# Four-step blocks of a decayed attention summed by VectorE's transposing reduction in place of TensorE's first burst

## The chip, the cores and the metric

One core of one Trainium2 chip. The metric is device time in microseconds (us) of one execution; profiles come from executions of the same program. PE is TensorE (PEld its weight loads), DVE is VectorE, ACT is ScalarE; L463 is line 463 of the kernel that the profile belongs to, so the same statement has another number in each kernel (L656, L706, L707 and L710 are all the MLP's first product).

## The reference

```python
# r, k, w, v: (4 batches, 8 heads, 768 steps, 48 channels)
for t in range(S):
    cur = u * k_t (x) v_t                     # outer product
    y_t = r_t . (state + cur)
    state = w_t[:, None] * state + k_t (x) v_t
# y as (3072, 384), then an MLP with exact Gelu:
out = gelu(y @ w_in) @ w_out                  # w_in (384, 2048), w_out (2048, 384)
```

## The kernel before

Time is cut into eight blocks, x = 0 to 7. For each, an attention part makes a matrix of r·k products with decays inside chunks of 64 steps, a state and y; an MLP then runs on y. The two are woven together: while the MLP of block x-1 runs, the attention of block x is taken forward by one piece at each "slot". The MLP's steps are 16 groups of six products (`h_ps`, each group followed by a Gelu), then the products with `w_out`. Only two banks hold `h_ps`, so group three needs the first Gelu.

From x = 2 on, the decayed products come in "quarters": at h = 1, 4 and 16, blocks of 4h steps are cut into four, and one burst of 96 matmuls makes the products between different quarters. The diagonal (step with itself) is a sum over channels on VectorE.

```python
QUARTERS = (1, 4, 16)
...
        if x >= 2:
            for q in range(qs):                                   # r * u * k, the diagonal
                nc.vector.scalar_tensor_tensor(out=kx[:, z], in0=r[:, z], scalar=u_sb[:, q:q + 1], in1=k[:, z], ...)
            nc.vector.tensor_reduce(out=diag_sb, in_=kx..., op=ALU.add, apply_transpose=True)
            yield
        # (cut) tot[2], tot[4], ...: products of w over 2, 4, ... steps
            def plain(h):                                         # copies of r into the right-hand side kx
                for z, f in ((s0[:, :, :, 0:h], 1), (s1[:, :, :, 0:h], 2), (s2, 3)):
                    nc.scalar.copy(out=z, in_=r4[:, :, :, f, :])
            def lay_out(h): ...                                   # two VectorE products, L442 and L443
            plain(1)
            lay_out(1)
            yield
            for h in QUARTERS:
                ...                                               # at h == 1: four small products place the diagonal (L456)
                            nc.tensor.matmul(d[...], lhsT=kc[...], rhs=rx[...], start=True, stop=True)   # the burst, L463
                nc.vector.tensor_mul(z, s0, ...)                  # r and k scaled for the next h
                ...
                        nc.vector.copy_predicated(out=an[...], mask=..., data=data)
                yield
...
        place = [...] if x == 1 else [0, 7, 11, 14, 16, 17, 17, 19, 20]      # steps for this block's pieces
        place_next = [40, 42] if x == 1 else [20, 22]                        # steps for the next block's preparation
```

## Time and profile before

| | before |
|---|---|
| median, lowest, highest (3 runs) | 626.23, 625.59, 627.41 us |
| span of the profiled run, granted clock | 625.5 us, 0.997 |
| PE / DVE / ACT busy | 97% / 70% / 30% |
| bursts of 96 matmuls, x = 2 to 7 | three a block, 2.14 us each |

### The profile page before, as it was taken

The numbers are of one execution on the slowest core, as the hardware profiler recorded it, in microseconds if no ns is written. First come the engines' busy times: TensorE is split into PE (matmuls) and PEld (weight loads), VectorE is DVE, ScalarE is ACT, GpSimd is POOL, SyncE is SP. The second block draws the span as 40 slices with busy tenths as digits, with TensorE's granted clock in tenths as the row PEclk, the third lists the DMA queues.
The fourth block names the chain that finished last, engine by engine and source line by source line (L and its number), as shares of the span: only waits on it lengthen the run. The fifth ranks groups of instructions, "written<-read, shape, count | busy, mean of one in ns | idle before, by whom it ended". The sixth has DMA issues, their size and how long they took to land.

```text
span 625.5 us, 16932 instructions
## 1 busy us (share of the span) xinstructions
PE 607.6 (97%) x7462; PEld 456.8 (73%) x7481; DVE 436.3 (70%) x802; ACT 186.0 (30%) x397; POOL 7.6 (1%) x29
## 2 busy tenths in 40 slices
PE   8798999989999999999999999999999999999997
PEld 4565666555689667996689667996689767995694
DVE  8987999798776777668776777677676777340120
ACT  2136556033224222223224232123234233112200
POOL 4000000000000000000000000000000000000000
PEclk9999999999999999999999999999999999999999
DMA  4576348002042214213042113212042002010001
GB/s 158 168 272 253 104 153 291 28 24 89 3 104 74 57 40 90 65 42 89 2 91 88 41 56 73 62 56 83 15 89 87 8 1 39 9 42 7 1 1 38
DMA packets 50505, 46.78 MB, mean 75 GB/s; under 512 B 31616, under 2 KB 35840, under 8 KB 50432
## 3 DMA queue, kind: packets, MB, share of 16 engines
q1 hardware_dynamic: 33120, 29.33, 14.8%
q10 hardware_dynamic: 17312, 16.37, 9.6%
q8 instruction: 59, 0.97, 0.6%
q14 instruction: 14, 0.11, 0.1%
HBM read 36.24 MB, written 4.72 MB: 65 GB/s over the span
## 4 chain that ended last, share of the span: by engine, by line
PE 81%; DVE 12%; issue 3%; DMA 2%; ACT 1%; SPq 0%; DVEq 0%; ACTq 0%
PE h_ps L656 35%; PE o_ps L676 29%; PE d L463 6%; PE o_ps L790 3%; DVE rkw L388 2%; PE d L353 2%; PE y_ps L571 2%; PE y_ps L589 2%; DVE e L291 2%; PE kv_ps L539 2%; DVE a_sb L396 1%; DMA raw<-in_w_in_dram 1%; PE warm L185 1%; DVE w_out_sb L295 1%; DMA xT<-ysb 1%
## 5 line engine op out<-in xcount | busy, mean ns | idle before, releaser
L656 PE MATMUL h_ps<-xT,w_in_sb 128*128 128x384 f32 x768 | 256.6, 491 | 0.4 <-DMA xT<-ysb 0.4
L656 PEld LDWEIGHTS h_ps<-xT,w_in_sb 128*128 128x128 f32 x768 | 144.3, 191 | 96.8 <-ACT xT L602 0.9
L659 ACT ACTIVATE g<-h_ps 128x384 f32<-128x384 f32 (+1 forms) x128 | 57.7, 451 | 216.4 <-PE h_ps L656 200.0
L494 DVE COPY_PREDICATED a_sb<-quarter,d 128x384 f32<-128x384 uint8 x162 | 82.4, 550 | 3.7
L676 PE MATMUL o_ps<-t,s 128*128 128x192 f32 x480 | 82.9, 329 | 0.0
L676 PEld LDWEIGHTS o_ps<-t,s 128*128 128x128 f32 x480 | 78.0, 190 | 0.8
L476 DVE TENSOR_TENSOR rkw<-rkw,tot_sb 128x768 f32<-128x768 f32 x18 | 17.3, 959 | 42.6 <-PE d L463 42.6
L463 PEld LDWEIGHTS d<-kx,rkw 64*64 64x64 f32 x1728 | 37.2, 135 | 9.1 <-issue 7.3
L463 PE MATMUL d<-kx,rkw 64*64 64x96 f32 x1728 | 40.7, 248 | 2.3 <-DVE kx L443 2.3
L790 PE MATMUL o_ps<-w_out_sb,g 128*128 128x384 f32 x128 | 42.7, 490 | 0.0
L437 ACT COPY kx<-rkw 128x384 f32<-128x384 f32 x54 | 31.3, 643 | 29.6 <-PE d L463 21.3
L676 PE MATMUL o_ps<-w_out_sb,g 128*128 128x192 f32 x224 | 39.3, 329 | 0.0
L676 PEld LDWEIGHTS o_ps<-w_out_sb,g 128*128 128x128 f32 x224 | 36.7, 190 | 2.2
L790 PEld LDWEIGHTS o_ps<-w_out_sb,g 128*128 128x128 f32 x128 | 23.9, 190 | 16.1 <-DVE o_sb L796 0.6
L669 DVE TENSOR_TENSOR s<-g 128x512 f32<-128x512 f32 x14 | 9.4, 672 | 29.9 <-ACT g L659 29.9
L676 PE MATMUL o_ps<-t,g 128*128 128x192 f32 x160 | 27.7, 327 | 0.2 <-ACT rkw L661 0.2
L676 PE MATMUL o_ps<-w_out_sb,s 128*128 128x192 f32 x160 | 27.6, 326 | 0.0
L353 PEld LDWEIGHTS d<-rkw 64*64 64x64 f32 x1152 | 18.7, 135 | 11.7 <-issue 5.8
L676 PEld LDWEIGHTS o_ps<-t,g 128*128 128x128 f32 x160 | 26.2, 190 | 0.5 <-ACT rkw L661 0.5
L676 PEld LDWEIGHTS o_ps<-w_out_sb,s 128*128 128x128 f32 x160 | 26.3, 190 | 0.0
L602 ACT COPY xT<-y_ps 48x384 f32<-48x384 f32 x46 | 21.7, 473 | 14.0 <-issue 12.4
L353 PE MATMUL d<-rkw 64*64 64x64 f32 (+1 forms) x1152 | 21.3, 222 | 4.4 <-DVE rkw L388 1.6
(109 smaller groups left out, 591.5 us busy)
## 6 DMA issues: line engine op xcount, KB each, us to landing
rkw<-in_rkw_dram ACTq DMA_DIRECT2D x45, 256.0 KB, 2.8
raw<-in_w_out_dram SPq DMA_DIRECT2D x8, 768.0 KB, 4.4
raw<-in_w_in_dram SPq DMA_DIRECT2D x7, 768.0 KB, 7.5
out_dram<-o_sb SPq DMA_DIRECT2D x21, 192.0 KB, 1.9
v_in<-in_v_dram ACTq DMA_DIRECT2D x5, 584.0 KB, 3.7
rkw<-in_rkw_dram SPq DMA_DIRECT2D x8, 288.0 KB, 3.6
rkw<-in_rkw_dram SPq DMA_DIRECT2D x9, 256.0 KB, 7.5
rkw<-kx SPq DMA_DIRECT2D x48, 48.0 KB, 2.1
```

The lines of the kernel that those rows point to most:

```text
L291: nc.vector.scalar_tensor_tensor(out=e, in0=hi, scalar=0x80000000, in1=e, op0=ALU.bitwise_and, op1=ALU.bitwise_or)
L353: nc.tensor.matmul(d[half[p], g, n * width:(n + 1) * width], lhsT=kc[half[g], b, i, p], rhs=right(half[g], b, i, p), start=True, stop=True)
L388: nc.vector.tensor_mul(rk, rk, tt)
L437: nc.scalar.copy(out=z, in_=r4[:, :, :, f, :])
L463: nc.tensor.matmul(d[half[p], g, i * 3 * C // 2:(i + 1) * 3 * C // 2], lhsT=kc[half[g], (n + i) // NI, (n + i) % NI, p], rhs=rx[half[g], 2 ...
L476: nc.vector.tensor_mul(z, z, t2[:, :, 1:2].to_broadcast(z.shape))
L494: nc.vector.copy_predicated(out=an[:, :, :, :, (a + 1) * h:], mask=mask.to_broadcast(data.shape), data=data)
L602: copy(out=xT[s, pair, :].rearrange("p (i c t) -> p c i t", c=2, t=C), in_=y[s])
L656: nc.tensor.matmul(h_ps, lhsT=w_in_sb[:, f // FI, j, f % FI * 128:(f % FI + 1) * 128], rhs=xT[:, j, :], start=(j == 0), stop=(j == NJ - 1))
L659: nc.scalar.activation(out=gs[group][:, f % FG, 0:t], in_=h_ps[:, 0:t], func=AF.Gelu)
L676: nc.tensor.matmul(o, lhsT=lhs(j), rhs=rhs(j), start=start and j == 0, stop=(j == HF - 1), skip_group_check=True)
L790: nc.tensor.matmul(o, lhsT=block(i, f // HF, f % HF), rhs=w_out_sb[:, f, :], start=(f == 0), stop=(f == NF - 1))
```

## The change

The intent: blocks of four steps are small enough that VectorE can make their ten products per block (step with itself, one, two and three steps apart) by multiplying shifted k and r and summing over channels with its transposing reduction. Eight small products put the sums in place. So the first burst is not needed, and `QUARTERS` starts at 4. The core of the diff:

```diff
-QUARTERS = (1, 4, 16)
+QUARTERS = (4, 16)
+FINE = 4
+        r4, k4, w4 = (z.rearrange("p (m a) -> p a m", a=FINE) for z in (r, k, w))
+        def transposed_sums(o, e, n):
+            nc.vector.tensor_reduce(out=fine_sb[:, e, 0:n]..., in_=kx[...], op=ALU.add, apply_transpose=True)
+        def apart(e, n):                                  # k times r, e steps apart
+            nc.vector.tensor_mul(kx[...].rearrange("p (a m) -> p a m", a=n), k4[:, 0:n], r4[:, e:e + n])
+        if x >= 2:
+            places_of = [apart(1, 3)]
+            times(k4[:, 0:2], w4[:, 1:3])
+            places_of.append(apart(2, 2))
+            times(k4[:, 0:1], w4[:, 2:3])
+            places_of.append(apart(3, 1))
+            yield
+            for e, place in enumerate(places_of, 1):
+                transposed_sums(place, e, FINE - e)
+            times(k4[:, 0:3], w4[:, 3:4]...)              # k and r scaled for h = 4
+            times(r4[:, 3:4], w4[:, 2:3])
+            times(r4[:, 1:2], w_0)
+            times(r4[:, 2:4], w_01...)
-            plain(1)
-            lay_out(1)
+            plain(FINE)
+            lay_out(FINE)
-                if h == 1:   # four small products for the diagonal
+                if h == FINE:
+                    for a in range(FINE):
+                        for g in range(2):
+                            nc.tensor.matmul(fine_ps[g][:, a * n_b:], lhsT=places[half[g], a], rhs=fine_sb[half[g], 0:FINE - a, a], ...)
# (cut) masks, and the predicated copies of the fine sums
-        place = [...] if x == 1 else [0, 7, 11, 14, 16, 17, 17, 19, 20]
+        place = [...] if x == 1 else [4, 9, 12, 14, 15, 15, 18, 19]
-        place_next = [40, 42] if x == 1 else [20, 22]
+        place_next = [34, 36, 38] if x == 1 else [20, 22, 24] if x % 2 == 0 else [20, 22, 27]
```

More of the change, by code (lines that the diff above doesn't have):

```diff
@@ L102 @@
     p1_alone = bufs[0][:, ALL + NF * 128:ALL + NF * 128 + DM // 2]
-    diag_sb = bufs[0][:, 3 * ALL - NP * T // 32:]
+    SPARE = ALL + NF * 128 + DM // 2
+    fine_sb = bufs[0][:, SPARE:SPARE + FINE * FINE * NPART * NI].rearrange("p (e a n) -> p e a n", e=FINE, a=FINE)
+    places = bufs[0][:, 3 * ALL - FINE * 128:].rearrange("p (a r) -> p a r", a=FINE)
     def load_first():
@@ L195 @@
     q_ints = [wk.tile([128, DM // 2], I32, name=name, bufs=1) for name in ("p1", "u2", "u3")]
-    s_qs = {h: q_ints[0][:, i * C:(i + 1) * C] for i, h in enumerate(QUARTERS)}
+    s_qs = {h: q_ints[0][:, i * C:(i + 1) * C] for i, h in enumerate((1,) + QUARTERS)}
     nc.gpsimd.iota(row, pattern=[[0, C]], base=0, channel_multiplier=1)
@@ L221 @@
     m_qs = {}
+    t_all, t_block = q_ints[1][:, 2 * C:3 * C], q_ints[2][:, 2 * C:3 * C]
+    nc.gpsimd.iota(t_all, pattern=[[1, C]], base=0, channel_multiplier=0)
+    nc.gpsimd.iota(t_block, pattern=[[1, C // FINE], [0, FINE]], base=0, channel_multiplier=0)
     for i, h in enumerate(QUARTERS):
@@ L228, with make_fine @@
             nc.gpsimd.iota(m_qs[h, a], pattern=[[4, C // 4 // h], [0, (3 - a) * h]], base=a, channel_multiplier=0)
+    fine_mask, later = (const.tile([128, C], U8, name=name) for name in ("fine_mask", "later"))
+    def make_fine():
+        nc.vector.tensor_tensor(out=fine_mask, in0=s_qs[FINE], in1=t_block, op=ALU.is_equal)
+        nc.vector.tensor_tensor(out=later, in0=t_all, in1=s_qs[1], op=ALU.is_ge)
+        nc.vector.tensor_tensor(out=fine_mask, in0=fine_mask, in1=later, op=ALU.bitwise_and)
+        nc.gpsimd.memset(places, 0.0)
+        for z in range(4):
+            o = slice(z * 32, (z + 1) * 32)
+            v = places[o]
+            v = bass.AP(tensor=v.tensor, offset=v.offset, ap=[v.ap[0], [128 + 1, FINE], [FINE, 32]])
+            nc.gpsimd.tensor_copy(out=v, in_=ident[o, o].unsqueeze(1).to_broadcast([32, FINE, 32]))
     def make_quarter_masks():
+        make_fine()
         for (h, a), m_q in m_qs.items():
@@ L235 @@
     make_identity(nc, ident)
-    both = const.tile([128, 2, C], F32, name="both")
-    nc.gpsimd.memset(both, 0.0)
-    for z in range(4):
-        o = slice(z * 32, (z + 1) * 32)
-        for i in range(2):
-            nc.gpsimd.tensor_copy(out=both[o, z // 2, i * 32:(i + 1) * 32], in_=ident[o, o])
     tot_sb = const.tile([128, NP * T], F32, name="tot_sb")
@@ L316, in attention @@
         xT = xT_of[x]
+        r4, k4, w4 = (z.rearrange("p (m a) -> p a m", a=FINE) for z in (r, k, w))
+        n_m = n_u // FINE
+        def transposed_sums(o, e, n):
+            nc.vector.tensor_reduce(out=fine_sb[:, e, 0:n].rearrange("p a n -> p (a n)"),
+                                    in_=kx[:, o:o + n * n_m].rearrange("p (m j) -> p m j", j=32),
+                                    axis=mybir.AxisListType.X, op=ALU.add, apply_transpose=True)
+        def apart(e, n):
+            o = sum(FINE - i for i in range(1, e)) * n_m
+            nc.vector.tensor_mul(kx[:, o:o + n * n_m].rearrange("p (a m) -> p a m", a=n), k4[:, 0:n], r4[:, e:e + n])
+            return o
         if x >= 2:
             for q in range(qs):
-                z = slice(q * T, (q + 1) * T)
-                nc.vector.scalar_tensor_tensor(out=kx[:, z], in0=r[:, z], scalar=u_sb[:, q:q + 1], in1=k[:, z],
+                m_q = slice(q * T // FINE, (q + 1) * T // FINE)
+                nc.vector.scalar_tensor_tensor(out=kx[:, 0:n_u].rearrange("p (a m) -> p a m", a=FINE)[:, :, m_q],
+                                               in0=r4[:, :, m_q], scalar=u_sb[:, q:q + 1], in1=k4[:, :, m_q],
                                                op0=ALU.mult, op1=ALU.mult)
-            nc.vector.tensor_reduce(out=diag_sb, in_=kx[:, 0:n_u].rearrange("p (m j) -> p m j", j=32), axis=mybir.AxisListType.X,
-                                    op=ALU.add, apply_transpose=True)
+            transposed_sums(0, 0, FINE)
             yield
@@ L342, in attention, with times @@
             at_tot += nb
-        if x < 2:
+        if x >= 2:
+            def times(z, by):
+                nc.vector.tensor_mul(z, z, by)
+            places_of = [apart(1, 3)]
[6 more added lines that the diff above has]
+                transposed_sums(place, e, FINE - e)
+            w_0, w_01 = w4[:, 0:1], tot[2].rearrange("p (m two) -> p two m", two=2)[:, 0:1]
+            times(k4[:, 0:3], w4[:, 3:4].to_broadcast([128, 3, n_m]))
+            times(r4[:, 3:4], w4[:, 2:3])
+            times(r4[:, 1:2], w_0)
+            times(r4[:, 2:4], w_01.to_broadcast([128, 2, n_m]))
+        else:
             yield
@@ L450, in quarters @@
                 banks = [ps.tile([128, 2, BANK], F32, name="d", tag="d", bufs=3) for _ in range(0, np_ * NI, 4)]
-                if h == 1:
-                    halves_of = diag_sb.rearrange("p (n c z) -> p n c z", c=2, z=2)
-                    for g in range(2):
-                        for c in range(2):
-                            nc.tensor.matmul(banks[-1][half[c], g, 6 * C:6 * C + 2 * np_ * NI], lhsT=both[:, g, :],
-                                             rhs=halves_of[:, :, c], start=True, stop=True)
+                if h == FINE:
+                    n_b = np_ * NI
+                    fine_ps = [banks[-1][:, g, 6 * C:6 * C + FINE * n_b] for g in range(2)]
+                    for a in range(FINE):
+                        for g in range(2):
+                            nc.tensor.matmul(fine_ps[g][:, a * n_b:], lhsT=places[half[g], a], rhs=fine_sb[half[g], 0:FINE - a, a],
+                                             start=(a == 0), stop=True, skip_group_check=True)
                 ds = []
@@ L495, in quarters @@
                         o += w_q
-                if h == 1:
-                    data = banks[-1][:, :, 6 * C:6 * C + 2 * np_ * NI].rearrange("p g (n z) -> p g n z", z=2)
-                    data = data.unsqueeze(4).to_broadcast([128, 2, np_ * NI, 2, C // 2])
-                    mask = masks[0].rearrange("p (z t) -> p z t", z=2).unsqueeze(1).unsqueeze(1)
-                    nc.vector.copy_predicated(out=at.rearrange("p g n (z t) -> p g n z t", z=2),
-                                              mask=mask.to_broadcast(data.shape), data=data)
+                if h == FINE:
+                    mask = fine_mask.rearrange("p (m b) -> p m b", b=FINE).unsqueeze(1)
+                    for g in range(2):
+                        data = fine_ps[g].rearrange("p (b n) -> p n b", n=n_b)
+                        data = data.unsqueeze(2).to_broadcast([128, n_b, C // FINE, FINE])
+                        nc.vector.copy_predicated(out=at[:, g].rearrange("p n (m b) -> p n m b", b=FINE),
+                                                  mask=mask.to_broadcast(data.shape), data=data)
                 yield
@@ L844 @@
     for x in range(1, NX):
-        place = [1, 2, 4, 7, 9, 11, 13, 15, 17, 20, 24, 32] if x == 1 else [0, 7, 11, 14, 16, 17, 17, 19, 20]
-        place_next = [40, 42] if x == 1 else [20, 22]
+        place = [1, 2, 4, 7, 9, 11, 13, 15, 18, 20, 26, 32] if x == 1 else [4, 9, 12, 14, 15, 15, 18, 19]
+        place_next = [34, 36, 38] if x == 1 else [20, 22, 24] if x % 2 == 0 else [20, 22, 27]
         loads = load(x + 1, nc.scalar if x > 1 else nc.sync)
-        times = range(20, 30) if x == 1 else (2, 3, 4, 5, 15, 16, 17, 19, 20, 21)
+        times = range(20, 30) if x == 1 else (2, 3, 4, 5, 13, 14, 15, 17, 18, 19)
         following = attention(x + 1, 0) if x + 1 < NX else iter(())
@@ L853 @@
         for step, _ in enumerate(mlp(x - 1)):
-            if x == 1 and step == 2 * NF + 2:
+            if x == 1 and step == 2 * NF - 4:
                 make_quarter_masks()
```

## The prediction

> **What bounds the kernel now.** I read the page's busy line first, then the chain that ended last in order of time, then VectorE's timeline around one hand-over between two time blocks, then durations by line.
>
> The busy line, then pieces of the chain (start, duration, engine, tile, line):
>
> ```profile
> PE 607.6 (97%) x7462; PEld 456.8 (73%) x7481; DVE 436.3 (70%) x802; ACT 186.0 (30%) x397; POOL 7.6 (1%) x29
> ```
> ```profile
> 137.03 0.97 DVE kx L443
> 138.13 3.06 PE d L463 x96
> ...
> 487.97 1.94 PE h_ps L656 x6
> 490.26 2.14 PE d L463 x96
> 492.40 13.74 PE h_ps L656 x42
> 506.14 2.14 PE d L463 x96
> 508.28 7.94 PE h_ps L656 x24
> 516.22 2.14 PE d L463 x96
> ```
>
> TensorE is busy 97% and from 138 us on the chain is TensorE nearly alone. So TensorE's work is the time there, and a change helps by what it takes off TensorE, as long as no other engine falls behind. Each of the six later blocks (x = 2 to 7) has three bursts of products, 2.14 us each, between groups of h_ps (6 instructions, 1.98 us a group). The change deletes the first burst. The one exception is the first hand-over, where TensorE waited for VectorE (L443) until 138.13.
>
> VectorE has 30% idle, but where it lies decides. Timeline of VectorE, around the hand-over at 488 us:
>
> ```profile
> 471.80 0.36 DVE L716 TENSOR_TENSOR u<-o_ps,p 128x192 f32<-128x192 f32 x1 [0.91 <-PE o_ps L676]
> ...
> 480.21 0.36 DVE L725 TENSOR_TENSOR u<-o_ps,p 128x192 f32<-128x192 f32 x1 [1.60 <-PE o_ps L676]
> 480.67 0.62 DVE L728 TENSOR_TENSOR o_sb<-o_sb,u 128x192 f32<-128x192 f32 x2
> 482.81 0.36 DVE L737 TENSOR_TENSOR o_sb<-o_ps,u 128x192 f32<-128x192 f32 x1 [1.51 <-PE o_ps L676]
> 483.09 0.95 DVE L341 TENSOR_TENSOR tot_sb<-rkw 128x768 f32<-128x768 f32 x1
> 484.07 1.71 DVE L341 TENSOR_TENSOR tot_sb<-tot_sb 128x384 f32<-128x384 f32 x5
> 485.69 0.86 DVE L442 TENSOR_TENSOR kx<-rkw 128x384 f32<-128x384 f32 x1
> 486.66 0.96 DVE L443 TENSOR_TENSOR kx<-kx,rkw 128x768 f32<-128x768 f32 x1
> ```
>
> The reader is to see that VectorE prepares the next block between the MLP's additions, and was done at 487.6, when TensorE wanted the result at 490.2: about 2.6 us to spare. Whatever is added between L716 and the first products of the next block has that room, no more.
>
> Last, one line of the kernel in its two forms, by source line (minimum/median/maximum ns): with steps of four elements (h = 1), and in runs of four or more.
>
> ```profile
> L442 DVE TENSOR_TENSOR kx<-rkw,tot_sb x12: 549/551/556, 143.1 to 510.2; 128x384 f32<-128x384 f32 x12
> L442 DVE TENSOR_TENSOR kx<-rkw,rkw x3: 831/861/866, 136.1 to 413.1; 128x384 f32<-128x384 f32 x3
> ```
>
> **What the Trainium skill says.** "VectorE: DVE Perf Modes", the perf-mode tier table: fp32 tensor_tensor and tensor_reduce run at one element per cycle. The trace agrees: 768 elements 0.96 us, 1152 1.35 us, a reduction of 1536 1.78 us. "SBUF — State Buffer", the cacheline note under Door 1: lines of 16 bytes, at least two hits per line for full rate. The pair above agrees: 855 against 552 ns for 384 elements that each lie in a line of their own, 0.79 ns more per element. Steps of two (L341, 0.95 us for 768) pay nothing. "TensorE: Matmul & The Clock Gate", Part 1: an idle TensorE drops to half clock and needs some 3.4 us of work to recover. The trace agrees: after 2.3 us without work at 138 the granted clock was 0.50 at 140.0 to 141.2, and that burst took 3.06 us, not 2.14; I book 1.7 us (3.4 at half) per long stall. "TensorEngine Tiling (Array Packing)", Instruction Overhead: a product of few columns costs some 60 cycles anyway; the four removed L456 products (8 instructions) took 0.34 us.
>
> **The change, part by part.** *TensorE, per block:* minus a burst (2.14) and L456 (0.34), plus eight small products (16 instructions, estimated 0.65 from L456's rate): -1.83 us. Six blocks: -11.0 us, all on the path.
>
> *VectorE, removed per block:* at h = 1, L442 0.86, L443 0.96, L470 1.35, L476 0.96, L479 0.96, nine predicated copies 6.4, L500 1.87: 13.4 us. *Added:* 16 x 384 = 6144 elements of products and scalings in nine instructions, all in steps of four: 6144 x 1.83 ns + 9 x 0.15 = 12.6 us (7.7 without the penalty); three more reductions, 2304 elements, 2.9; L322 in steps of four, 4 x 0.91 for 4 x 0.61, +1.2; two copies of 768, some 2.5. Sum 19.2, so about +6 us per block. VectorE would still be only some 85% busy; the total is harmless.
>
> *What moves is not.* The removed 13.4 us lay mostly after the first burst, under h_ps groups. The added work lies before the next block's products. In the built order ScalarE's three copies into kx (which used to read unscaled r) now wait for the last scaling of r, and stand ahead of the first Gelu of the next MLP. h_ps has two banks, so group three waits for that Gelu. The deadline is thus not the fine products after group five but group three.
>
> Reckoning for a hand-over after an odd MLP (x to 3, 5, 7), zero at the end of the product that L716 adds. TensorE: state products 1.44, five products of 2.6: 14.4; two groups: 18.4, then it needs the Gelu. VectorE: L716 and two subtractions 1.6; u-product 4 x 0.91 + 1.78: 7.0; L725 and L728: 8.0; L737 (its product ends 9.2): 9.6; totals 2.6, products 2.26 + 1.57 + 0.86, scalings 1.57 + 0.86: 19.3; the output's addition 19.7, which also holds bank two, so group two runs 19.7 to 21.7; reductions 2.9, k 2.26, r 0.86 + 0.86 + 1.57: 28.2. ScalarE: copies 1.34, Gelu 0.49: 30.0. TensorE is late by 30.0 - 18.4 = **11.6 us**; without the stride penalty 25.2 - 18.4 = 6.8.
>
> After an even MLP (x to 4, 6) the middle piece stands ahead of an addition that frees an accumulator: that product waits until 22.1, not 17.0 (5.1), and group three until 38.2, not 31.3 (6.9): **12.0** (6.9 without).
>
> First hand-over: VectorE is free of the weights' conversions at 117.05 as before; masks 1.0, subtractions 2.7, evictions to 122.0, subtractions 125.7, u-product 131.0, one subtraction and totals 134.4, products and scalings 141.5, reductions 144.4, k and r 150.0, ScalarE 152.0. TensorE's first group ends at 135.8: 16.2 stalled against 2.3 before. Less 2.75 of burst (3.06 + 0.34 - 0.65), plus 1.7 of clock: **+12.9** (+6.8 without).
>
> Sum: 12.9 + 3 x (11.6 + 1.7) + 2 x (12.0 + 1.7) - 5 x 1.83 = 12.9 + 39.9 + 27.4 - 9.2 = +71: 697 us. Without the penalty +40: 667.
>
> **Rivals.** (1) *TensorE's saving shows whole:* 626 - 11 = 615. For it: 97% busy, and moved slots suggest someone fitted the work. Against: even at one element per cycle the VectorE chain above is 25.2 us where 18.4 fit. (2) *Waits and saving cancel:* bare VectorE work in that chain, with no waits in between and no penalty, is 20.7, plus 1.8 of ScalarE: 22.5, so at least 4.1 late against 1.83 saved; with the first hand-over that gives some 640. This is my floor if the order is right. (3) *The stride costs more*, say because writes in place pay too: 0.5 ns x 3840 elements is 2 us more per hand-over, 710. (4) *The tail binds:* kv now follows the last burst after six groups (11.9 us), where before it had 13.3; the transposed k's moves take about 10. I expect under 1 us.
>
> **Range and chances.** Between 667 and 697, nearer the second because the penalty is measured on the same operation with the same step, but only on one line: **688 us**, range 650 to 710. Faster by 2% needs the deadline reading to be wrong altogether: 0.03. Within 2% (to 638.7): 0.05. Slower: 0.92.
>
> **What would show it.** Right: TensorE's busy share falls to some 88 to 92%; gaps before h_ps groups two and three at every hand-over, with VectorE's scalings and ScalarE's kx copies as releasers; scalings of 768 elements at 1.5 to 1.6 us; d products at 1152 instructions; granted clock halved after each gap. Wrong: strided products at 0.96 us per 768 (then 667 or less), or a chain that is TensorE alone (then 615).

## More of the kernel before

TensorE's timeline at the hand-over at which block 3's preparation ends and its work begins (start, duration, engine, line, operation, count; a bracket would tell idle time and its releaser):

```profile
204.16 2.10 PE L656 MATMUL h_ps<-xT,w_in_sb 128*128 128x384 f32 x6
206.19 0.42 PE L456 MATMUL d<-rkw,both 128*64 128x24 f32 x8
206.53 2.21 PE L463 MATMUL d<-kx,rkw 64*64 64x96 f32 x96
208.68 13.81 PE L656 MATMUL h_ps<-xT,w_in_sb 128*128 128x384 f32 x42
```

The reader is to see that no line has a bracket: TensorE waits for nothing, and the first burst stands between group one and group two. This is what the change wants to save.

## The result

| | before | after |
|---|---|---|
| median (lowest to highest), 4 runs each | 626.49 (625.59 to 627.41) us | 703.75 (702.68 to 707.82) us |
| ratio, 95% interval | 1 | 1.1245 [1.1197, 1.1293] |
| span of the profiled run, granted clock | 625.5 us, 0.997 | 702.3 us, 0.942 |

A ratio is the mean time of one kernel's runs over that of the other's of the same rounds, so it is not quite the ratio of the medians that are quoted. Executions in which one die ran at a lower clock are left out of the means. The changed kernel is correct and 77 us slower.

The page after the change: the busy line, TensorE's granted clock in 40 slices, and the chain that ended last, by engine.

```profile
PE 626.7 (89%) x6953; PEld 458.8 (65%) x6953; DVE 464.3 (66%) x796; ACT 169.5 (24%) x379; POOL 8.4 (1%) x24
...
PEclk9999999969998799988999699997999879999999
...
PE 66%; DVE 26%; ACT 4%; issue 3%; ACTq 0%; DVEq 0%
```

TensorE's share fell from 97% to 89%, although its busy time rose: 576 burst matmuls are gone, and yet it is 19 us longer busy, because after these gaps it runs at a lower clock (the 6s, 7s and 8s of the second line; at the hand-over shown below the granted clock was 0.50 from 223.0 to 225.2 and from 231.2 to 236.0 us). VectorE now holds a quarter of the chain. The waits say where (engine and line that waited, what it waited for, total us, times, longest):

```profile
ACT kx L485 <- DVE rkw L375: 104.0, 6, 19.8
...
PEld h_ps L706 <- ACT rkw L711: 30.2, 6, 15.4
```

Six times, once for each block, ScalarE's three copies into kx (L485) waited for VectorE's scalings of r (L375), 17 us in the mean. ScalarE executes in order (the Trainium skill, "Perfetto Trace Analysis", the note under Tensor Engine Instruction, calls ACT and DVE strict FIFO; the next lines agree), so the Gelu behind the copies waits as well, and TensorE's next group of `h_ps` for the Gelu. One hand-over in the three timelines: VectorE, ScalarE, TensorE.

```profile
224.23 3.72 DVE L375 TENSOR_TENSOR rkw<-rkw 128x1152 f32<-128x1152 f32 x3
227.84 1.53 DVE L375 TENSOR_TENSOR rkw<-rkw,tot_sb 128x768 f32<-128x768 f32 x1
```
```profile
229.41 1.34 ACT L485 COPY kx<-rkw 128x384 f32<-128x384 f32 x3 [15.08 <-DVE rkw L375]
230.65 0.86 ACT L709 ACTIVATE g<-h_ps 128x384 f32<-128x384 f32 x2
```
```profile
216.41 2.10 PE L706 MATMUL h_ps<-xT,w_in_sb 128*128 128x384 f32 x6
221.76 3.37 PE L706 MATMUL h_ps<-xT,w_in_sb 128*128 128x384 f32 x6 [3.25 <-DVE o_sb L803]
231.19 8.59 PE L706 MATMUL h_ps<-xT,w_in_sb 128*128 128x384 f32 x18 [6.06 <-ACT g L709]
```

Group one ran at 216.4; group two waited 3.25 us for an addition (L803) that VectorE could do only after its fine products; group three waited 6.06 us for the Gelu behind the copies. Group three started 14.8 us after group one, where two groups at full clock take some 4. The three groups from 231.2 took 8.59 us; the same 18 matmuls at full clock took 6.07 (in e9_scalar below), so 2.5 us were lost to the clock. After an even MLP there are again two stalls:

```profile
303.29 5.16 PE L726 MATMUL o_ps<-t,s 128*128 128x192 f32 x16 [4.34 <-DVE u L814]
...
310.88 4.03 PE L706 MATMUL h_ps<-xT,w_in_sb 128*128 128x384 f32 x12
320.92 8.10 PE L706 MATMUL h_ps<-xT,w_in_sb 128*128 128x384 f32 x18 [6.01 <-ACT rkw L711]
```

A product that takes some 2.8 us elsewhere waited 4.34 us for L814 and took 5.16; group three waited 6.01 us and its row took 8.10. The other even hand-over has the same two waits (4.36 and 6.06 us) with 4.55 and 7.99.

### The profile page after: what moved, and what is told of

It is laid out like the page before. It is cut to its first block, busy times and chain, and to the rows that moved or that the text cites. A ratio compares the mean times of both kernels' runs of the same rounds, so it can differ in the third digit from the quotient of the medians.

```text
span 702.3 us, 15827 instructions
## 1 busy us (share of the span) xinstructions
PE 626.7 (89%) x6953; PEld 458.8 (65%) x6953; DVE 464.3 (66%) x796; ACT 169.5 (24%) x379; POOL 8.4 (1%) x24
## 4 chain that ended last, share of the span: by engine, by line
PE 66%; DVE 26%; ACT 4%; issue 3%; ACTq 0%; DVEq 0%
PE h_ps L706 29%; PE o_ps L726 22%; DVE rkw L375 6%; PE d L512 4%; DVE kx L346 4%; DVE tot_sb L371 2%; PE warm L189 2%; DVE rkw L339 2%; DVE rkw L436 2%; ACT rkw L573 2%; DVE e L306 2%; PE y_ps L639 2%; PE kv_ps L589 2%; PE d L401 2%; PE y_ps L621 2%
## 5 line engine op out<-in xcount | busy, mean ns | idle before, releaser
L706 PE MATMUL h_ps<-xT,w_in_sb 128*128 128x384 f32 x768 | 274.3, 515 | 53.1 <-ACT rkw L711 26.9
L706 PEld LDWEIGHTS h_ps<-xT,w_in_sb 128*128 128x128 f32 x768 | 150.8, 200 | 163.6 <-ACT rkw L711 30.2
L726 PEld LDWEIGHTS o_ps<-t,s 128*128 128x128 f32 x480 | 81.7, 198 | 10.1 <-DVE u L814 9.3
L525 DVE TENSOR_TENSOR rkw<-rkw,tot_sb 128x768 f32<-128x768 f32 x12 | 11.5, 959 | 68.7 <-PE d L512 68.7
L543 DVE COPY_PREDICATED a_sb<-quarter,d 128x384 f32<-128x384 uint8 (+2 forms) x108 | 44.9, 436 | 2.5
L485 ACT COPY kx<-rkw 128x384 f32<-128x384 f32 x36 | 16.0, 508 | 119.9 <-DVE rkw L375 104.0
L375 DVE TENSOR_TENSOR rkw<-rkw 128x384 f32<-128x384 f32 (+2 forms) x24 | 32.2, 1364 | 0.4
L401 PEld LDWEIGHTS d<-rkw 64*64 64x64 f32 x1152 | 18.9, 136 | 12.3 <-issue 6.0
L339 DVE TRANSPOSE_TENSOR_REDUCE rkw<-kx 128x48 f32<-128x1536 f32 (+3 forms) x24 | 26.8, 1154 | 0.2
L512 PE MATMUL d<-kx,rkw 64*64 64x96 f32 x1152 | 26.5, 245 | 0.0
L512 PEld LDWEIGHTS d<-kx,rkw 64*64 64x64 f32 x1152 | 24.3, 133 | 3.4 <-DVE a_sb L550 1.6
```

What stands on the lines that cost most here:

```text
L339: nc.vector.tensor_reduce(out=fine_sb[:, e, 0:n].rearrange("p a n -> p (a n)"), in_=kx[:, o:o + n * n_m].rearrange("p (m j) -> p m j", j=3 ...
L375: nc.vector.tensor_mul(z, z, by)
L401: nc.tensor.matmul(d[half[p], g, n * width:(n + 1) * width], lhsT=kc[half[g], b, i, p], rhs=right(half[g], b, i, p), start=True, stop=True)
L512: nc.tensor.matmul(d[half[p], g, i * 3 * C // 2:(i + 1) * 3 * C // 2], lhsT=kc[half[g], (n + i) // NI, (n + i) % NI, p], rhs=rx[half[g], 2 ...
L543: nc.vector.copy_predicated(out=an[:, :, :, :, (a + 1) * h:], mask=mask.to_broadcast(data.shape), data=data)
L706: nc.tensor.matmul(h_ps, lhsT=w_in_sb[:, f // FI, j, f % FI * 128:(f % FI + 1) * 128], rhs=xT[:, j, :], start=(j == 0), stop=(j == NJ - 1))
```

## The experiments

Theory: the change takes work off TensorE (some 1.5 to 1.8 us a block), but puts VectorE's chain, and ScalarE's copies behind it, ahead of a deadline that TensorE meets at each hand-over; the time is lost in those gaps. Rivals: the fine products cost too much wherever they stand; the step of four elements alone is the cause; what is added before a hand-over is hidden anyway, so something else is.

Runs listed in one heading shared a chip. Where not said otherwise a kernel is correct.

### The stride, and ScalarE's copies (e1_dense, e2_vec_copies)

e1_dense makes the three views read runs instead of steps of four. Its results are wrong; the work is the same in elements and order.

```diff
-        r4, k4, w4 = (z.rearrange("p (m a) -> p a m", a=FINE) for z in (r, k, w))
+        r4, k4, w4 = (z.rearrange("p (a m) -> p a m", a=FINE) for z in (r, k, w))
```

> The changed kernel with the four-step views read densely (wrong result on purpose: the same instructions and element counts, no steps of 16 bytes). Theory (the stride is a part of the late chain): L346, L352 and L375 fall to 1.35 us for 1152, 0.96 for 768, 0.55 for 384, 0.61 for L352; that is 5.9 us less in each of the six chains, each stall of TensorE shorter by as much, total 664 us (655 to 672), still well slower than before. Rival 1 (the stride does not matter, only the order of the instructions does): over 695. Rival 2 (the stride is the whole cause): under 630.

Measured: 671.31 us (2 runs), ratio 1.0701 [1.0636, 1.0767]. Products of 1152 elements took 1.35 us, not 2.25. Its TensorE at the same hand-over:

```profile
210.91 2.10 PE L706 MATMUL h_ps<-xT,w_in_sb 128*128 128x384 f32 x6
213.64 2.20 PE L706 MATMUL h_ps<-xT,w_in_sb 128*128 128x384 f32 x6 [0.63 <-DVE o_sb L803]
221.04 7.55 PE L706 MATMUL h_ps<-xT,w_in_sb 128*128 128x384 f32 x18 [5.20 <-ACT g L709]
```

Group three still starts 10.1 us after group one. So the step of four elements accounts for some 32 of the 77 us (34 by the ratios), and without it the kernel would still be 45 us slower than before: the rival "the stride alone" falls.

e2_vec_copies leaves the stride, and does the three copies on VectorE, so that ScalarE's Gelus are free of them.

```diff
+                copy = nc.vector.tensor_copy if h == FINE else nc.scalar.copy      # (shortened)
-                    nc.scalar.copy(out=z, in_=r4[:, :, :, f, :])
+                    copy(z, r4[:, :, :, f, :])
```

> The changed kernel with the three copies into kx ahead of the first Gelu done by VectorE instead of ScalarE, so that the first Gelu of the next MLP no longer waits for the last scaling of r. Theory (the deadline is group three, set by ScalarE's order): after the second hand-over groups three to five run under VectorE's chain, TensorE gains some 8 us at each of five hand-overs, 2 us at the first (there the third bank is still held by the eviction L846 that stands behind the chain); total 660 us (650 to 672). Rival (VectorE's amount of work is what binds and the order on ScalarE is indifferent): 700 to 708, since VectorE gets a little more work.

Measured: 663.71 us (2 runs), ratio 1.058 [1.0516, 1.0644], though VectorE got more work. TensorE at the hand-over, where group one started at 214.34:

```profile
219.72 10.99 PE L707 MATMUL h_ps<-xT,w_in_sb 128*128 128x384 f32 x24 [3.28 <-DVE o_sb L804]
```

The wait before group three is gone: groups two to five are one row. What is left at this hand-over is the wait of group two, and its clock: 10.99 us for 24 matmuls that take 8.0 at full clock. One queue's order was worth 40 us in this kernel.

### Does work before a hand-over cost its length? (e3_dose2, e4_dose8)

To the kernel before, two or eight idle products of 768 elements (0.96 us each, into a buffer that nobody reads) are added after the totals of w, for x >= 2.

```diff
+        if x >= 2:
+            for _ in range(2):          # e4_dose8: range(8)
+                nc.vector.tensor_mul(bufs[0][:, 3776:4544], w[:, 0:768], w[:, 768:1536])
```

> The kernel before with two dummy products of 768 elements (1.9 us of VectorE) put between the totals and the first layout of each block x >= 2, nothing else. Theory (2.6 us of room at each later hand-over, none at the first): +2 us (0.5 to 4), all of it at the first hand-over. Rival (VectorE's total load counts, 6 x 1.9): +11 us.

Measured: 631.53 us (4 runs), ratio 1.007 [1.0023, 1.0116], about 4 us: the top of what was expected, and not all of it at the first hand-over.

> As before with eight dummies (7.7 us per block, about what the change adds to the chain net of clock). Theory: TensorE waits at every hand-over: +8 at the first, some 5 to 7 plus 1.5 to 2.5 of lowered clock at each of the five others: +45 us (35 to 55), though the products of the finest quarters are all still there and no new kind of instruction is. Rival (VectorE has 30% idle, so 46 us of extra work hides): under +15.

Measured: 675.77 us (2 runs), ratio 1.0772 [1.0707, 1.0837], about 48 us. In its trace, at the hand-over after an odd MLP:

```profile
213.03 0.42 PE L459 MATMUL d<-rkw,both 128*64 128x24 f32 x8
218.75 4.12 PE L466 MATMUL d<-kx,rkw 64*64 64x96 f32 x96 [5.30 <-DVE kx L446]
```

Eight products are 7.7 us; the burst waited 5.30 us, so some 2.4 us were hidden, as the 2.6 us of room in the prediction said; and it ran at half clock (4.12 us where the same row has 2.21 in the kernel before; granted clock 0.50). Two doses fit into that room at the later bursts and cost where there is none: at the first hand-over (its burst waited 4.16 us in e3_dose2, 2.30 before), and twice 1.2 us at a product that, after an even MLP, waits for an addition on VectorE. There eight doses cost 7.17 us of waiting, so only some 0.7 us are free: this deadline comes before the burst's. So a few us of VectorE's work, with no change to TensorE's, cost as much as they exceed the room plus the clock. "Hidden anyway" falls.

### Order of access, and the slots (e5_order, e6_slots, e7_all)

e5_order turns the loops round: rows of a block inside, blocks outside, so that neighbours are taken one after the other.

```diff
+            rm, km, wm = (z.rearrange("p (m a) -> p m a", a=FINE) for z in (r, k, w))
-            nc.vector.tensor_mul(kx[...].rearrange("p (a m) -> p a m", a=n), k4[:, 0:n], r4[:, e:e + n])
+            nc.vector.tensor_mul(kx[...].rearrange("p (a m) -> p m a", a=n), km[:, :, 0:n], rm[:, :, e:e + n])
-            times(k4[:, 0:2], w4[:, 1:3])
+            times(km[:, :, 0:2], wm[:, :, 1:3])
# (cut) the same for the u-product and for the other scalings; r's rows 1 and 3 in one instruction
```

> The kernel after with only the order of iteration changed: blocks outside, the four rows of a block inside, so that neighbouring elements are taken one after the other. In-place scalings read and write lines of four elements together; products and the u-product read together and write scattered (384 elements apart). Correct. My theory (the penalty of a step of four elements is paid for the order of access, not for the layout): scalings of 768 at 0.96 us, not 1.52 to 1.57; of 1152 at 1.35, not 2.21; products of 1152 at 1.35 if a scattered write of single elements is free, at 2.2 if it pays like a strided read; u-product pieces at 0.55 to 0.6 if free. The chain to group three is then 2.9 us shorter per hand-over if writes pay (total some 680), up to 6 us shorter if they do not (some 665, near the 671 of the contiguous variant). Rival (the layout itself costs, whatever the order): nothing changes, 700 or more.

Measured: 692.54 us (2 runs), ratio 1.1052 [1.101, 1.1093]. Durations by line (minimum/median/maximum ns, forms) of the products that now read runs and write scattered:

```profile
L347 DVE TENSOR_TENSOR kx<-rkw,rkw x9: 837/1507/2187, 133.9 to 461.3; 128x1152 f32<-128x1152 f32 x3, 128x768 f32<-128x768 f32 x3, 128x384 f32<-128x384 f32 x3
```

In the changed kernel the same three forms took 834/1514/2252: scattered writes pay as strided reads do. The scalings in place, where both sides are friendly now, run at full rate (768 elements 0.96 us). At the hand-over group three started 12.1 us after group one, 2.6 us sooner than in the changed kernel, as expected for the case in which writes pay; the total fell only 11 us where I had reckoned some 23. The waits are not the reason: at every one of the six hand-overs they are 2.6 to 2.9 us shorter than in the changed kernel, 16 us in all (after an even MLP 0.7 at the product, 1.9 at group three). Part of that went into slower clock afterwards: the 24 matmuls after the first stall took 10.96 us for 10.10, the 18 at the second and third odd hand-over 8.85 and some 8.7 for 7.83 and 7.64. And 23 was more than six times the 2.9 us that the expectation itself named.

e6_slots takes e2's copies and e5's scalings, cuts the preparation into five slots instead of three, puts them where VectorE waits for products anyway, and moves six of eight subtractions of weights (L683, 0.95 us each) from the first hand-over into the next MLP.

```diff
+            yield                       # after the first fine product and scaling
+            yield                       # after the reductions
-        place_next = [34, 36, 38] if x == 1 else [20, 22, 24] if x % 2 == 0 else [20, 22, 27]
+        place_next = [31, 33, 35, 47, 47] if x == 1 else [17, 20, 21, 22, 24] if x % 2 == 0 else [17, 20, 22, 24, 27]
-            next(more, None)
+            if step in ((29, 30) if x == 1 else range(4, 10)):
+                next(more, None)
# (cut) the copies of e2, the scalings of e5, and the line that carries `more` into the next MLP
```

> The kernel after with three repairs: the three copies of kx on VectorE, in-place scalings in the friendly order, and five slots in place of three, put where VectorE waits for products anyway, with the conversion's subtractions moved off the first hand-over. Correct. My theory (the change loses by where the work stands, and TensorE is the bound again once VectorE is ready in time): each of six blocks saves 2.14 + 0.34 - 0.99 = 1.5 us against the kernel before, 617 us (612 to 625), with TensorE busy over 96% and a granted clock of 0.98 or more. Rival (the fine products or VectorE's larger sum of work cost inherently, slots or not): not below 640.

Measured: 621.98 us (4 runs), ratio 0.9923 [0.9892, 0.9953], clock 0.997. The fine blocks are not too dear in themselves: with VectorE 73% busy, more than in any kernel so far, the time is not above that of the kernel before, and by the interval 0.5 to 1.1% below it. The rival falls.

e7_all adds e5's order for the products too.

> The run before with the products and the u-product in the friendly order of reading too (writes scattered). Correct. If scattered writes are free, VectorE has 3 us less per block ahead of the hand-over and what waits were left there go: 2 to 6 us below the run before, or the same if none were left. If scattered writes pay as reads do, the same time.

Measured: 620.79 us (4 runs), ratio 0.9906 [0.9876, 0.9936]: the same within the intervals. What it still lost is seen between the last groups and the key-value products (kv_ps):

```profile
237.16 0.33 PE L593 MATMUL kv_ps<-v_in,rkw 64*64 64x48 f32 x6
237.75 1.59 PE L593 MATMUL kv_ps<-v_in,rkw 64*64 64x48 f32 x90 [0.27 <-ACT rkw L577]
```

### The key-value slot, and the slots without the copies (e8_kv, e9_scalar)

e8_kv is e7_all with the key-value products one MLP product later: behind the first product of the MLP's second half (in the kernel before they stand behind the second).

```diff
-        place = [...] if x == 1 else [4, 9, 12, 14, 15, 15, 18, 19]
+        place = [...] if x == 1 else [4, 9, 12, 14, 16, 16, 18, 19]
```

> The kernel e7_all with the key-value products and the state's additions one product later (two slots 15 to 16, so that they follow the first product of the MLP's second half instead of standing ahead of it). Correct. In e7_all they waited for ScalarE's copies of the transposed k, 0.2 to 0.3 us seen as idle of TensorE per block and 0.54 us per two blocks as longer busy time. If that wait is a cost of the moved slots, it goes: 1.5 to 4 us below e7_all (ratio to the kernel before 0.985 to 0.988). If VectorE's fences or the next block's u-product become late instead, the same or up to 3 us more.

Measured: 616.22 us (6 runs; 615.20 to 619.34), ratio 0.984 [0.9809, 0.9872], slightly better than expected (1.5 to 4 us below e7_all; the medians differ by 4.6). It is the fastest kernel. Its page and its hand-over:

```profile
PE 599.4 (97%) x6934; PEld 447.6 (73%) x6953; DVE 450.8 (73%) x808; ACT 162.5 (26%) x361; POOL 8.4 (1%) x24
```
```profile
200.50 9.84 PE L710 MATMUL h_ps<-xT,w_in_sb 128*128 128x384 f32 x30
210.27 1.06 PE L509 MATMUL d<-rkw 64*128 64x48 f32 x16
211.27 2.21 PE L516 MATMUL d<-kx,rkw 64*64 64x96 f32 x96
```

No bracket is left. Five groups, then the eight small products (16 instructions), then the burst at h = 4: this is what the change was meant to be. From the hand-over at 204.16 to the one two blocks later, at 346.22, the kernel before took 142.1 us; e8_kv took 139.0 (200.5 to 339.5). The difference, 3.0 us for two blocks, is the saving of 2.14 + 0.34 - 0.99 = 1.49 us a block, whole.

e9_scalar is e7_all with the copies back on ScalarE.

> The kernel e7_all with the three copies of kx back on ScalarE, ahead of the first Gelu: all other repairs kept. Correct. It tells whether the slots alone would have been enough. In e7_all the last scaling of r ends at 204.0 and group three starts at 204.3; with the copies (1.34) and a Gelu (0.49) behind the scaling group three starts at 205.9, late by 1.5 us, plus up to 1 us of clock, at five hand-overs, and something at the first: 627 to 640, most likely 632. If the order on ScalarE is what mattered and the slots little, 655 or more; if the slots alone suffice, under 624.

Measured: 637.53 us (4 runs), ratio 1.0172 [1.0143, 1.02].

```profile
211.81 1.34 ACT L489 COPY kx<-rkw 128x384 f32<-128x384 f32 x3 [5.92 <-DVE rkw L376]
```
```profile
213.59 6.07 PE L710 MATMUL h_ps<-xT,w_in_sb 128*128 128x384 f32 x18 [1.52 <-ACT g L713]
```

Group three is late by 1.52 us, as reckoned (1.5), and 5.6 us after group one. So the slots, the order of access and the moved subtractions together bring 66 us with the copies left on ScalarE, and ScalarE's order is still worth 17 us with them (40 without). How the 66 us divide among the three was not measured. At the first hand-over it waited 5.45 us for ScalarE, more than I had allowed for, which puts the time at the high end of the range.

### What the old kernel could have had too (e10_before_subs)

The kernel before, with e6's move of six subtractions only.

```diff
-        more = iter(())
+        more = more if x == 2 else iter(())
-            next(more, None)
+            if step in ((35, 36) if x == 1 else range(4, 10)):
+                next(more, None)
```

> The kernel before, with only one of the repairs that the repaired kernel got: six of the eight subtractions of weights (L629, 0.92 us each) moved from the first hand-over into the next MLP. Correct. It tells what of the repaired kernel's gain the old kernel could have had as well. The old kernel stalls there 2.3 us for VectorE and loses some 0.9 us of clock in the burst: 2.5 to 4 us to gain, 623 us (ratio 0.993 to 0.997). If VectorE is short elsewhere in the next block, the same 626. The repaired kernel's 616 then keeps 6 to 8 us that belong to the finest blocks themselves.

Measured: 623.42 us (6 runs), ratio 0.9957 [0.9939, 0.9975]. So, if the move brings as much in e8_kv, 2.7 of its 10 us have nothing to do with fine blocks; some 7 us do.

Group three's start after group one's, at the hand-over after the MLP of block 1, sums up the series (medians beside it; before has a burst between and is left out):

| kernel | group one to group three | time |
|---|---|---|
| after | 14.8 us | 703.75 us |
| e5_order | 12.1 | 692.54 |
| e1_dense (wrong) | 10.1 | 671.31 |
| e9_scalar | 5.6 | 637.53 |
| e8_kv | no gap (some 4) | 616.22 |

## Why the prediction was right, point by point

- **The bound and the deadline: right.** TensorE alone was the time before; the doses showed that VectorE's room before a burst is some 2.5 us and that what exceeds it costs its length. They also showed less room, 0.7 us, at the product after an even MLP, which the prediction's 2.6 us did not mention for the old kernel.
- **Copies ahead of the Gelu, two banks: right.** Reckoned: group three 30.0 us after the zero point; measured 29.3 (L766 at 201.89, group three at 231.19). e2_vec_copies took the copies out of that queue and got 40 us back.
- **The stride: right.** Strided products and scalings took 1.52 to 1.56 us for 768 elements. The prediction put the penalty at 30 us (697 against 667); e1_dense measured 32. The agreement is in part luck: the sum without the penalty (25.2 us) left out the four pieces of the u-product (0.91 against 0.61 us, 1.2 us a hand-over), with which the penalty is some 37. In e1_dense the waits shrank by 4.6 to 5.7 us a hand-over, less than the 6 us by which VectorE's chain did.
- **Odd hand-overs: right.** Reckoned 11.6 us late and 1.7 of clock, 13.3; measured 14.8 - 3.9 = 10.9 and 2.5, 13.4. At the other two the wait was the same and the clock cost less: 12.6 and 12.5.
- **First hand-over: right.** Reckoned +12.9 net. The next block's first group starts at 216.41 instead of 204.16: +12.3. (The wait itself was 14.8 us where 16.2 was reckoned, with 1.5 us more at a product before it.)
- **Even hand-overs: mechanism right, the clock mis-sized.** The waits were 4.34 + 6.01 = 10.4 us where 12.0 was reckoned. I booked one loss of clock of 1.7 us; there are two stalls, and each has its own: the product took 5.16 us for 2.8, group three's row 8.10 for 6.07. Together 4.4 us, and 3.7 at the other even hand-over.
- **Saving: mis-sized.** The small products took 0.99 us a block on the chain, not 0.65, so 1.49 us were saved and not 1.83.
- **The tail (rival 4): mis-sized.** "Under 1 us" was too little if it meant all blocks: from the last six groups of `h_ps` to the next product of y, block 3 took 22.07 us in the changed kernel and in e7_all, and 21.50 in e8_kv, 0.6 us a block and some 3 in all.
- **The sum: short by 6 us, with errors both ways.** Put together from the traces: 12.3 (first), 38.5 (three odd), 28.8 (two even), -7.5 (saving), +2.9 (tail of five blocks): +75. The prediction's sum was +71 (697), measured +77; 2 us stay unexplained. Clock, saving and tail were reckoned too low, the waits too high. The 688 leaned to the lower side for a doubt about the stride that the runs don't support.
- **The other rivals fell.** Rival 2 expected some 640; even without the stride the kernel took 671. Rival 3, that writes in place pay too, would have shown in the scalings: in place they took 1.53 us for 768 elements, the products 1.52. "The saving shows whole" is what e8_kv does (with 616 against 615 reckoned, helped by the subtractions), but only once the slots, the copies and the order are mended.

Not settled: how much of e6_slots' step is the new slots and how much the moved subtractions; in the old kernel the latter brought 2.7 us.

## What to carry to other kernels

When work is moved from a bound engine to a half-idle one, look not at the idle share but at the deadlines: which result must be ready when the bound engine comes past, and what stands in the same queues ahead of it. A short instruction (here 1.34 us of copies) in an in-order queue ahead of the bound engine's feeder makes that engine wait for everything the instruction waits for. And before giving up such a change, move the pieces into the waits that the timeline of the helping engine shows: here the same idea went from 12% slower to 1.6% faster, of which 0.4% is a repair that the old kernel could have had too.

## What the Trainium skill lacked or had wrong

- "SBUF — State Buffer", the cacheline note under Door 1, says that there is a penalty but not its size. Measured on VectorE in fp32 with steps of four elements: 2.25 us for 1152 elements where runs take 1.35, about 0.8 ns an element. It does not say either whether reads or writes pay: strided reads (2.25), scattered writes (2.18) and both in place (2.21) pay once, the same.
- No page that I found has the same for ScalarE's copies: at h = 1 (single elements in steps of four) the three of block 2 took 0.911 to 0.935 us, in runs of four 0.505 to 0.513 for the same 384 elements.
- No page that I found has the cost of predicated copies by pattern: nine copies of the same sizes took 6.42 us at h = 1 (single elements) and 3.95 at h = 4.
- "TensorE: Matmul & The Clock Gate", Part 1, says that what is issued in the first 3.4 us or so after an idle stretch runs at half clock and everything after at full, which would be 1.7 us lost; it also says that the window runs freely, so that this varies, and gives some 4 us with a spread of 0.5 for a kernel's start. Losses here were 1.5 us (e1_dense, after 5.2 us idle), 2.5 (after, 6.06 us idle) and 3.0 (e2_vec_copies, 3.28 us idle; granted clock 0.50 from 219.7 to 225 us and 0.61 in the next): stretches at half clock of some 3, 5 and 6 us, twice the loss, and not in proportion to the gap. After 1.52 us idle (e9_scalar) the 18 matmuls ran at full rate.
- "TensorEngine Tiling (Array Packing)", Instruction Overhead, gives the floor of a small product, and from the removed products I took a rate of 0.34 us for eight instructions. Sixteen of 12 to 48 columns in tiles of 64x128 took 0.99 us on the chain, with a weight load of 0.19 us each (the loads overlap). Which of the two sets the pace was not measured.
